# A fused FFT and expert kernel: late tiles by seven quarter products, result scatters in a queue of their own, gates zeroed first

## The chip, the cores and the metric

The kernel runs on one core of a Trainium2 chip. The metric is the device time of one execution in microseconds. A profiled execution comes with it: its span is the time from the first to the last recorded instruction, and the execution's own time is a little longer.

## The reference

Eight batches of 2496 tokens, 256 values each, are first filtered along the sequence with a Fourier transform, and the result goes through a mixture of eight experts, one expert a token, none dropped.

```python
X = np.fft.rfft(x, axis=1)
Y = X * (filt_r + 1j * filt_i)[None, :, :]
x = np.fft.irfft(Y, n=2496, axis=1).reshape(19968, 256)

logits = x @ w_gate                        # 256 x 8
expert_idx = np.argmax(logits, axis=1)
gate_w = softmax(logits)[arange(N), expert_idx]
for e in range(8):                         # rows of one expert
    h = np.maximum(x[rows of e] @ w1[e], 0.0)   # 256 -> 1024
    y[rows of e] = h @ w2[e]                    # 1024 -> 256
return gate_w[:, None] * y
```

All is float32. A float32 matmul appears in the profile as two MATMUL instructions, each with its LDWEIGHTS.

## The kernel before

The transform is a prime-factor one: 2496 = 39 x 64. For each batch, `stage_a` multiplies by the table tas (tile fin in, zo out, stored to zd in DRAM), `stage_b` by tbs and then by the filter ht (tiles ys and yw), `stage_c` by tcs (uo out, stored to ud) and `stage_d` by tds (yo out). The first batch stays in SBUF and is turned by TensorE instead (`first_a`, `turn_z`, `first_c`, `turn_u`; tiles zt, ut, zi, ui). The imaginary filter parts are multiplied by signs on GpSimd: `load_filters` lists the parts in `signs`, and `turn_z` works the list off. The gate weights lie in two padded tiles, wg (for the logits of batches 0 to 2) and wb (for the later ones); `load_rest`, one step at 0.8 of slot 0, zeroes them on VectorE and loads them, the row ids and the valid mask through the Sync queue. `make_constants` runs before all steps.

`route` finds each token's expert and its place among the expert's rows, and `scatter` writes the row with its id and gate to the DRAM tile rows by an indirect DMA of GpSimd. After each batch `tile_map` cuts the new rows into tiles of 512, 256 or 128 rows of one expert each: 65 tiles, of which 28 have 512 rows (tiles 1 and 7 to 33), then eight of 256 (34 to 41) and 23 of 128 (from `SHORT` = 42; `PLACE` = 34).

A tile's first product (x by w1, relu, into the two tiles hT) has two halves, one w1 transfer each. For 512 rows and for the last batch's 256 rows it is done `hidden_by_quarters`: seven products of quarters in the place of eight, with sums of x (`turn_x`, tile sums) and of w1 (`w1_sums`, tile wsum) made on GpSimd and the outputs added up on VectorE. The second product is `result(i, j)`: for each 128 rows, eight matmuls of 128 x 128 by 128 x 256, one scaling by the gate on VectorE or ScalarE into ys (four buffers), and at once an indirect DMA on GpSimd, which scatters the 128 rows into the output. It takes w2 from w2t (two buffers, one for each half) or, from tile `PLACE` on, from w2s, which holds all of w2. In the last batch `result` also issues the pad scatters of `pad_rows`, one a call.

The order of all instructions on each engine is written out by a planner when the program is built. The class `Order` keeps a clock for each engine and an estimate of when each tile is ready. The main loop picks the next step for TensorE among the open transform steps and the heads of two streams, `first_products` and `second_products`; `when(key)` says when a head could start. Two streams that are both ready alternate. After each step `flush` issues stores that are due, `more_loads` the transform's loads, `side` the routing work, and `prefetch` the expert tiles' rows and weights and the w1 sums. The odd half of tile i's first product waits until the second product of tile i - 1 is over (`ends`). When the transform and the routing are over, `late` is filled: the transform's SBUF is given back and w2s and eight more w1 buffers (w1b) are placed there; w2s loads start at once. Each engine and each queue works its instructions off in the order in which they were issued. All instructions pass through the helper `Issue`, so nearly every one carries line 243.

Of the kernel before, what the change touches and what calls it, by code (L numbers as in the profile page):

```python
# [124 lines left out]
class Order:  # L125
# [5 lines left out]
    def __init__(self, nc):  # L131
        self.nc = nc
        self.t = dict.fromkeys(("tensor", "vector", "scalar", "gpsimd", "sync", "transfers"), 0.0)
        self.slow = self.busy = self.last = 0.0
        self.lands = [0.0] * 8
        self.done, self.used, self.slots, self.ahead = {}, {}, {}, {}
        self.tensor, self.vector, self.scalar, self.gpsimd, self.sync = (
            Issue(self, name) for name in ("tensor", "vector", "scalar", "gpsimd", "sync"))
# [37 lines left out]
        return size / n * packet / 14e3 * (1.7 if n >= 1024 and (in_ if out.space == DRAM else out).ap[0][1] <= 64 else 1.0)  # L176

    def count(self, engine, op, args, named):
        aps = [a for a in list(args) + list(named.values()) if isinstance(a, bass.AP)]
        if not aps:  # L180
            return
        out, ins = aps[0], aps[1:]
        if "out" in named:
            out = named["out"]
            ins = [a for a in aps if a is not out]
        if op.endswith("value_load"):
            out, ins = None, aps
        at = named.get("out_offset")
        if at is not None:
            ins.append(at.ap)  # L190
        kept = [a for a in ins if a.space != DRAM or a.name[:2] in ("zd", "ud")]
        free = self.t[engine]
        start = max([free] + [self.ready(a) + (self.HOP if engine != "sync" else 0.0) for a in kept])
        if out is not None:
            start = max(start, self.ahead.pop(out.name, 0.0))
            n = int(np.prod([d[1] for d in out.ap][1:])) if out.space != DRAM else 0
        tail = 0.0
        if op.endswith("dma_start"):
            busy = 1.03 if engine == "gpsimd" else 0.4
            if engine == "sync":  # L200
                start = max(start, self.lands[-8])
            self.t[engine] = start + busy
            took = self.transfer(out, named["in_"])
            self.t["transfers"] = max(self.t["transfers"], start + busy) + took
            end, tail = self.t["transfers"], self.LOAD
            if engine == "sync":
                self.lands = self.lands[-7:] + [end + tail]
        else:
            if out is None:
                took = 0.8 if engine == "sync" else 0.02  # L210
            elif engine == "tensor":
                if start > self.busy + 1.2:
                    self.slow = start + 3.4
                rows = out.ap[0][1]
                took = max(0.1, 0.00085 * n) if op == "transpose" else max(0.216, 0.00169 * n) if rows > 32 else 0.00045 * n
                took *= 2.0 if start < self.slow else 1.0
                tail = 0.25
            elif engine == "vector":
                took = 0.15 + n / 960
            elif engine == "scalar":  # L220
                took = 0.16 + n / 1200
            else:
                took = 0.2 + n / 480
            end = self.t[engine] = start + took
            if engine == "tensor":
                self.busy = end
        for a in kept:
            self.used[a.name] = max(self.used.get(a.name, 0.0), end)
        for key in self.parts(out) if out is not None else ():
            self.done[key] = max(self.done.get(key, 0.0), end + tail)  # L230
        self.last = end + tail
# [59 lines left out]
def kernel(  # L291
# [86 lines left out]
    vld = cst.tile([P, 2 * NG + 2], F32, name="vld")  # L378


    first = ExitStack()
    pro = open_pool(first, name="pro", bufs=2, side="right")
    tau_i = pro.tile([1, 32], I32, name="tau_i", bufs=1)
    e_i = pro.tile([P, E], I32, name="e_i", bufs=1)
# [49 lines left out]

    def load_rest():
        nc.sync.dma_start(out=tds, in_=td)
        nc.vector.memset(wg, 0.0)
        nc.sync.dma_start(out=wg[:, :, :E], in_=moe_w_gate.rearrange("(i p) e -> p i e", p=P))
        nc.vector.memset(wb, 0.0)
        for i in range(4):  # L440
            nc.sync.dma_start(out=wb[i * CT:(i + 1) * CT, :, i * E:(i + 1) * E], in_=moe_w_gate.rearrange("(j p) e -> p j e", p=CT))
        nc.sync.dma_start(out=ids0, in_=ids)
        nc.sync.dma_start(out=vld, in_=valid)

    def make_constants():
        make_identity(nc.nc, ident)
        nc.gpsimd.memset(ones, 1.0)
        nc.gpsimd.affine_select(
# [30 lines left out]
    NIN, YB = 7, 6  # L479
    sb.live["in"] = lambda: {tile.name for tile in ins.values()}  # L480

    moves, stored = [], set()

    def move(o, i):
        moves.append((i, lambda: nc.sync.dma_start(out=o, in_=i)))
# [4 lines left out]
    def flush():  # L490
        while moves and (moves[0][0] is None or nc.ready(moves[0][0]) <= t["tensor"] + 0.2):
            moves.pop(0)[1]()

    def fin(key):
        ins[key] = sb.tile([P, 4, D], F32, tag="in", name="fin", bufs=NIN)
# [128 lines left out]
    def turn_z(f):  # L624
        if f % 4 == 0:
            nc.scalar.copy(out=ht[HP:, f:f + 4], in_=ht[:HP, f:f + 4])
            while signs and signs[0][0] <= f // 4:
                _, part, sign = signs.pop(0)
                nc.gpsimd.tensor_tensor(part, part, sign, op=ALU.mult)
        zi = outs["zi", f] = pro.tile([P, 2, D], F32, tag="zi", name="zi")  # L630
# [219 lines left out]
            yield  # L850

    def scatter(key, at, what):
        sc = nc.gpsimd.indirect_dma_start(
            out=rowsd,
            out_offset=bass.IndirectOffsetOnAxis(ap=at, axis=0),
# [10 lines left out]
    def tile_map(b, rows, n, last):  # L866
# [19 lines left out]
        yield 3  # L886
        most = max(m for group in GROUPS for _, m in group)
        tau = pools["moe"].tile([1, most], F32, tag="tau", name="tau", bufs=1)[:, :n]
        past = pools["moe"].tile([P, D], F32, tag="ys", name="past", bufs=4)[0:1, :n * (E - 1)].rearrange("p (n e) -> p n e", e=E - 1)
        she = (1, n, E - 1)  # L890
        nc.vector.tensor_tensor(
# [39 lines left out]
    SHORT = next(i for i in range(NT) if TILES[i][0] == 1)  # L931

    PLACE = next(i for i in range(NT) if TILES[i] == (2, B - 1))
    late = {}

    def quarters(i):
# [23 lines left out]
    def weights(h, second):  # L960
# [10 lines left out]
            return  # L971
        ev = nc.sync.value_load(work[i][1], min_val=0, max_val=E - 1)
        if second:
            w2t[h] = pools["moe"].tile([P, FH2, D], F32, tag="w2t", name="w2t", bufs=2)
            nc.sync.dma_start(out=w2t[h], in_=moe_w2[bass.ds(ev, 1), k].rearrange("o p i d -> p (o i) d"))
        else:
            pool, bufs = (late["w1"], 8) if i >= SHORT else (pools["moe"], 3)
            w1t[h] = pool.tile([P, DH, 2, 2 * P], F32, tag="w1t", name="w1t", bufs=bufs)
            nc.sync.dma_start(out=w1t[h], in_=moe_w1[bass.ds(ev, 1), k].rearrange("o p i h f -> p (o i) h f"))
# [89 lines left out]
    def result(i, j):  # L1069
# [5 lines left out]
        p = bank()  # L1075
        for k in range(FT):
            w2 = late["w2s"][:, bass.ds(ev, 1), k, :] if i >= PLACE else w2t[2 * i + k // FH2][:, k % FH2, :]
            mm(p[:, :D], lhsT=hs[i][k % 4 // 2][:, k // 4, k % 2, j * P:(j + 1) * P], rhs=w2, start=(k == 0), stop=(k == FT - 1))
        ys = pools["moe"].tile([P, D], F32, tag="ys", name="ys", bufs=4)
        gate = gis[i][:, j, 8:9]  # L1080
        either(p, D, lambda: nc.vector.tensor_scalar(ys, in0=p[:, :D], scalar1=gate, scalar2=None, op0=ALU.mult),
               lambda: nc.scalar.activation(ys, p[:, :D], AF.Copy, scale=gate))
        nc.gpsimd.indirect_dma_start(
            out=out,
            out_offset=bass.IndirectOffsetOnAxis(ap=gis[i].bitcast(U32)[:, j, :1], axis=0),
            in_=ys,
            in_offset=None,
            bounds_check=N - 1,
            oob_is_err=False,
        )  # L1090


    sides = []

# [116 lines left out]
    def prefetch():  # L1211
# [6 lines left out]
        for what in ("w1", "w2"):  # L1218
            h = got[what]
            if h < 2 * min(len(work), NT - RARE) and rows_at[work[h // 2][3]] <= t["tensor"] and (  # L1220
                    h - used[what] < ((3 if h < 2 * SHORT else 8) if what == "w1" else 2 if h < 2 * PLACE else 8)):
                weights(h, what == "w2")
                asked.add((what, h))
                got[what] += 1
        for h in range(used["w1"], got["w1"]):
            if quarters(h // 2) and h not in wsum and len(wsum) < 2 and nc.ready(w1t[h]) <= max(t["tensor"], t["gpsimd"]) + 0.3:
                w1_sums(h)

    def when(key):

# [2 lines left out]
        if what == "w2":  # L1233
            if halves[0] <= n or key not in asked:
                return None
            return max(ps.free("bank"), nc.ready(*hs[i], *((late["w2s"],) if i >= PLACE else (w2t[2 * i], w2t[2 * i + 1]))))
        if key not in asked or what != "x" and n % 2 and ends[0] < i:
            return None
        if what == "x":
# [44 lines left out]
    def second_products():  # L1284

        for i in range(NT - RARE):
            for j in range(TILES[i][0]):
                yield lambda: result(i, j), 3.42, ("w2", 2 * i + 1)
            hs.pop(i), gis.pop(i), w2t.pop(2 * i, None), w2t.pop(2 * i + 1, None)
            used["w2"] += 2  # L1290
            ends[0] += 1

    def rare_tiles():

        for i in range(NT - RARE, NT):
# [4 lines left out]
            for h in (2 * i, 2 * i + 1):  # L1300
                for a in range(4):
                    hidden(i, h % 2, a)
            result(i, 0)

    def share():

# [5 lines left out]
    with tc.manual_schedule(engines=None):  # L1312
# [35 lines left out]
        while fs or any(heads):  # L1348
# [27 lines left out]
            if not fs and not sides and not late:  # L1376
                fft.close()
                tail = late["tail"] = open_pool(ctx, name="tail", bufs=1)
                late["w1"] = open_pool(ctx, name="w1b", bufs=8)
                late["n"] = 0  # L1380
                late["pads"] = pad_rows()
                late["w2s"] = tail.tile([P, E, FT, D], F32, name="w2s")
            prefetch()
            if used["x"] > SHORT and "need" not in late:
                late["need"] = nc.values_load(need, min_val=0, max_val=GROUPS[-1][-1][1])
        with tc.If(late["need"] > GROUPS[-1][-1][1] - RARE):  # L1386
            rare_tiles()

# [29 lines left out]
```

## Time and profile before

| | us |
|---|---|
| median of 3 runs | 1496.89 (1492.83 to 1498.1) |
| the profiled execution's own time | 1495.25 |
| its span | 1493.5 |
| TensorE busy (matmul) | 1456.2 |
| VectorE busy | 767.1 |
| GpSimd busy | 732.0 |
| ScalarE busy | 471.5 |

A row of the profile names engine, operation, the tile written and the tiles read, the shapes and the number of instructions; then busy time, mean duration, and the idle time before such instructions with what ended it. Busy time of TensorE counts overlapping instructions once. PEld is its weight load, SPq the Sync engine's DMA queue, POOL is GpSimd, DVE VectorE, ACT ScalarE.

### The profile page before, as it was taken

What the parts mean: (1) busy time and instruction counts of PE and PEld (TensorE: products, weight loads), DVE (VectorE), ACT (ScalarE), POOL (GpSimd) and SP (SyncE); (2) the same over time, 40 slices, a digit from 0 to 9 for tenths busy, and PEclk for the clock granted to TensorE, in tenths of its full rate; (3) what the DMA queues carried; (4) which work ended last, traced back from release to release, by engine and by line L of the source; (5) the groups of instructions that cost most, each with busy time, mean ns of one, the idle gap of its engine ahead of it and who ended that gap; (6) DMA issues with size and microseconds to landing.
All of it is one profiled execution on the core that took longest, in us unless ns stands there. A gap on an engine that the chain in (4) does not pass through costs nothing. (4 is left out here: it accounts for less than half of the span.)

```text
span 1493.5 us, 24437 instructions
## 1 busy us (share of the span) xinstructions
PE 1456.2 (98%) x7396; PEld 1149.4 (77%) x7396; DVE 767.1 (51%) x1731; ACT 471.5 (32%) x984; POOL 732.0 (49%) x1053
## 2 busy tenths in 40 slices
PE   8898999999999999999999999999999999999998
PEld 6453556767677767777778788887888889999997
DVE  4567669255765665567756545437344344441110
ACT  4454542333332233322222322222222222223332
POOL 3434455355545554555466565664546455741111
PEclk9899999999999999999999999999999999999999
DMA  9649898787875576547355535545455543356661
GB/s 262 203 150 326 288 324 265 229 272 224 293 213 175 153 266 179 161 130 251 106 138 167 176 113 143 125 150 150 149 178 172 170 146 107 112 190 178 182 180 51
DMA packets 216376, 278.10 MB, mean 186 GB/s; under 512 B 124131, under 2 KB 163708, under 8 KB 216245
## 3 DMA queue, kind: packets, MB, share of 16 engines
q1 hardware_dynamic: 197125, 233.19, 52.4%
q0 software_dynamic: 19120, 43.33, 8.4%
q8 instruction: 62, 1.02, 0.3%
q14 instruction: 69, 0.57, 0.1%
HBM read 196.45 MB, written 80.64 MB: 186 GB/s over the span
## 5 line engine op out<-in xcount | busy, mean ns | idle before, releaser
L243 PE MATMUL bank<-w2t,hT 128*128 128x256 f32 x1984 | 446.4, 381 | 1.0 <-DVE hT L243 1.0
L243 DVE TENSOR_TENSOR hT<-bank,hT 128x512 f32<-128x512 f32 (+1 forms) x504 | 300.9, 626 | 277.9 <-PE bank L243 157.8
L243 PEld LDWEIGHTS bank<-w2t,hT 128*128 128x128 f32 x1984 | 376.2, 191 | 64.2 <-issue 10.6
L243 POOL DMA_INDIRECT out_dram<-ys,ng x161 | 160.7, 998 | 473.4 <-ACT ys L243 181.0
L243 PE MATMUL bank<-xT,w1t 128*128 128x256 f32 (+1 forms) x1728 | 316.6, 329 | 0.0
L243 PEld LDWEIGHTS bank<-xT,w1t 128*128 128x128 f32 x1728 | 267.2, 192 | 30.8 <-issue 6.5
L243 ACT ACTIVATE hT<-hT 128x1024 f32<-128x1024 f32 (+1 forms) x144 | 134.6, 960 | 375.1 <-DVE hT L243 364.1
L243 POOL DMA_INDIRECT rows<-yo,row x176 | 180.5, 1026 | 68.5 <-POOL yo L243 28.7
L243 ACT ACTIVATE ys<-bank,ng 128x256 f32<-128x256 f32 x121 | 57.4, 474 | 365.3 <-PE bank L243 311.0
L243 PE MATMUL bank<-sums,wsum 128*128 128x256 f32 (+1 forms) x576 | 135.7, 358 | 0.0
L243 PE MATMUL bank<-w2s,hT 128*128 x592 | 132.6, 379 | 0.0
L243 PEld LDWEIGHTS bank<-w2s,hT 128*128 128x128 f32 x592 | 110.3, 190 | 13.8
L243 PEld LDWEIGHTS bank<-sums,wsum 128*128 128x128 f32 x576 | 100.9, 190 | 20.0 <-issue 9.6
L243 DVE TENSOR_TENSOR ys<-bank,ht 128x512 f32<-128x512 f32 x80 | 54.9, 686 | 64.4 <-PE bank L243 59.8
L243 PE MATMUL bank<-fin,tas 117*120 117x512 f32 x154 | 77.7, 624 | 10.5 <-DMA fin<-in_x_dram 9.9
L243 DVE STREAM_TRANSPOSE xT<-xg 128x512 f32<-128x512 f32 (+2 forms) x126 | 57.5, 495 | 57.1 <-PE bank L243 56.1
L243 PE MATMUL bank<-fin,tds 120*128 120x512 f32 (+1 forms) x168 | 74.9, 565 | 4.3 <-DMA fin<-ud 4.1
L243 PE MATMUL bank<-ys,tcs 128*128 128x512 f32 x140 | 73.9, 613 | 4.1 <-DVE yw L243 3.4
L243 POOL TENSOR_TENSOR wsum<-w1t 128x256 f32<-128x256 f32 x72 | 53.6, 745 | 48.6 <-PE bank L243 45.7
L243 PE MATMUL bank<-fin,tbs 128*128 128x512 f32 x140 | 73.4, 611 | 2.0 <-DMA fin<-zd 2.0
L243 ACT ACTIVATE hT<-bank 128x128 f32<-128x128 f32 (+1 forms) x191 | 57.7, 304 | 53.0 <-PE bank L243 45.0
L243 PE MATMUL bank<-xT,wsum 128*128 128x256 f32 (+1 forms) x288 | 68.9, 362 | 1.9 <-DVE hT L243 1.9
(150 smaller groups left out, 1492.7 us busy)
## 6 DMA issues: line engine op xcount, KB each, us to landing
w1t<-in_moe_w_dram SPq DMA_DIRECT2D x126, 512.0 KB
w2t<-in_moe_w_dram SPq DMA_DIRECT2D x68, 512.0 KB
fin<-in_x_dram SPq DMA_DIRECT2D x39, 512.0 KB
fin<-zd SPq DMA_DIRECT2D x35, 512.0 KB
ud<-uo SPq DMA_DIRECT2D x35, 512.0 KB
fin<-ud SPq DMA_DIRECT2D x35, 512.0 KB
zd<-zo SPq DMA_DIRECT2D x35, 480.0 KB
xg<-rows SPq DMA_DIRECT2D x112, 128.0 KB
```

The source lines that it names most:

```text
L243: return real(*args, **named)
```

## The change

It has four parts.

First, the second product of a 512-row tile that begins when `late` is filled is made by `result_by_quarters`: the product 512 x 1024 by 1024 x 256 is cut into two halves of rows, of the inner dimension and of columns, and seven products of quarters (two times four matmuls of 128 columns each) take the place of eight. `h_sums` makes the sums of hT on VectorE (three adds of 128 x 1024; a fourth in the steps), `w2_sums` those of w2 on GpSimd (four of 128 x 512, one at a time between other work). Outputs are added up on VectorE and scaled on ScalarE. w2t gets two more buffers in a pool `quads`, which is closed after the last such tile (`LARGE` = 34) and whose place w1b then takes. The host lays w2 out so that the first half of the inner dimension is the first half of hT; `result` reads hT in that order for all tiles.

Second, `result` no longer issues its scatter: `deliver` puts it into a list, and `send` issues it when the planner takes the rows to be ready, or when more than three wait. Output scatters are declared free of order among themselves. Where a scatter would directly follow another on GpSimd, a memset of one element's width goes between them.

Third, the zeroing of wg and wb moves from `load_rest` to the start of `make_constants`.

Fourth, `turn_z` applies the signs of one more group of filter rows.

```diff
     def load_rest():
         nc.sync.dma_start(out=tds, in_=td)
-        nc.vector.memset(wg, 0.0)
         nc.sync.dma_start(out=wg[:, :, :E], ...)
-        nc.vector.memset(wb, 0.0)
...
     def make_constants():
+        nc.vector.memset(wg, 0.0)
+        nc.vector.memset(wb, 0.0)
         make_identity(nc.nc, ident)
...
     def flush():
...
+        while sends and (nc.ready(sends[0][0]) <= t["tensor"] + 0.2 or len(sends) > 3):
+            send()
...
-            while signs and signs[0][0] <= f // 4:
+            while signs and signs[0][0] <= f // 4 + 1:
...
     def scatter(key, at, what):
+        if nc.sent:
+            nc.gpsimd.memset(tau0[:, 31:], 0.0)
...
+            w2t[h] = (late["quads"] if late and late["flip"] else pools["moe"]).tile([P, FH2, D], F32, tag="w2t", name="w2t", bufs=2)
...
-        nc.gpsimd.indirect_dma_start(out=out, ...)
+        deliver(i, j, ys)
+
+    def send():
+        ys, ng, j = sends.pop(0)
+        if nc.sent:
+            nc.gpsimd.memset(tau0[:, 31:], 0.0)
+        sc = nc.gpsimd.indirect_dma_start(out=out, ...)
+        tc.declare_no_dep(sc.ins, group="results", reason="rows of their own")
+        tc.add_to_no_dep_group("results", sc.ins)
...
+    def h_sums(i):
+        a = [t.rearrange("p f v (r c) -> p r (f v) c", r=2) for t in hs[i]]
+        ss = hsum[i] = [late["quads"].tile([P, FH2, 2 * P], F32, tag="hsum", name="hsum", bufs=3) for _ in range(2)]
+        nc.vector.tensor_tensor(ss[0], a[0][:, 1], a[1][:, 1], op=ALU.add)
+        nc.vector.tensor_tensor(ss[1], ss[0], a[0][:, 0], op=ALU.subtract)
+        nc.vector.tensor_tensor(a[0][:, 1], a[0][:, 0], a[0][:, 1], op=ALU.subtract)
+
+    def w2_sums(i):
+        w = [w2t[2 * i + g].rearrange("p k (n d) -> p n k d", n=2) for g in range(2)]
+        ts = late["quads"].tile([P, 3, FH2, P], F32, tag="tsum", name="tsum", bufs=2)
+        nc.gpsimd.tensor_tensor(ts[:, 0], w[0][:, 1], w[0][:, 0], op=ALU.subtract)
+        yield
+        nc.gpsimd.tensor_tensor(ts[:, 1], w[1][:, 1], ts[:, 0], op=ALU.subtract)
+        yield
+        nc.gpsimd.tensor_tensor(ts[:, 2], w[1][:, 0], ts[:, 1], op=ALU.subtract)
+        yield
+        nc.gpsimd.tensor_tensor(w[0][:, 1], w[1][:, 1], w[0][:, 1], op=ALU.subtract)
+        tsum[i] = ts
+
+    def result_by_quarters(i):
...
+        def product(left, right):
+            q = bank()[:, :D].rearrange("p (j d) -> p j d", j=2)
+            for j in range(2):
+                for k in range(FH2):
+                    mm(q[:, j], lhsT=left[:, k, j * P:(j + 1) * P], rhs=right[:, k], start=k == 0, stop=k == FH2 - 1)
+            return q
...
+        q = product(a[0][:, 0], w[0][:, 0])
+        nc.scalar.copy(out=one, in_=q)
+        yield
+        q = product(a[1][:, 0], w[1][:, 0])
+        add(top[:, :, 0], q, one)
+        yield
+        ss, ts = hsum[i], tsum[i]
+        q = product(ss[1], ts[:, 1])
+        add(two, q, one)
+        nc.vector.tensor_tensor(a[1][:, 0], a[1][:, 0], ss[1], op=ALU.subtract)
+        yield
+        q = product(a[0][:, 1], w[0][:, 1])
+        add(three, q, two)
+        yield
+        q = product(ss[0], ts[:, 0])
+        add(low[:, :, 1], q, three)
+        add(four, q, two)
+        yield
+        q = product(a[1][:, 1], ts[:, 2])
+        add(low[:, :, 0], q, three)
+        for j in range(2):
+            send(2 + j, low[:, j])
+        yield
+        q = product(a[1][:, 0], w[1][:, 1])
+        add(top[:, :, 1], q, four)
+        for j in range(2):
+            send(j, top[:, j])
+        yield
...
     def second_products():
         for i in range(NT - RARE):
+            if late and i < LARGE:
+                wide.add(i)
...
+                for j in range(7):
+                    yield go, 1.79, ("wide", 2 * i + 1)
+            else:
...
             ends[0] += 1
+            if ends[0] == LARGE:
+                quads.close()
```

In `result_by_quarters` the inner `send(j, y)` takes a ys buffer, scales on ScalarE and calls `deliver`. `prefetch` issues `h_sums` once both hT tiles of the tile are ready, and one step of `w2_sums` at a time, for the tile at hand or the next, when GpSimd's clock is not more than 0.5 us ahead of TensorE's.

## The prediction

> **What bounds the kernel now.** I read the page first, then windows of the late stage, then TensorE's order of time at both ends of the run, then the waits of the places where TensorE stood still.
>
> ```profile
> PE 1456.2 (98%) x7396; PEld 1149.4 (77%) x7396; DVE 767.1 (51%) x1731; ACT 471.5 (32%) x984; POOL 732.0 (49%) x1053
> PEclk9899999999999999999999999999999999999999
> DMA  9649898787875576547355535545455543356661
> ```
>
> TensorE is busy for 98% of the span, so time falls only if TensorE gets less work or loses one of its few gaps. Those gaps (about 37 us) lie before 320 us, around 1014 to 1033 us and after the last matmul at 1487 us. The third digit of the DMA row (75 to 112 us) is slack, the next four are not.
>
> The late stage, in TensorE's order of time (start and duration in us, then the instruction and how many):
>
> ```profile
> 1220.61 1.05 PE L243 MATMUL bank<-xT,w1t 128*128 128x128 f32 x8
> ...
> 1223.29 0.61 PE L243 MATMUL bank<-xT,wsum 128*128 128x128 f32 x4
> 1223.74 13.98 PE L243 MATMUL bank<-w2t,hT 128*128 128x256 f32 x64
> 1237.55 1.05 PE L243 MATMUL bank<-xT,w1t 128*128 128x128 f32 x8
> ```
>
> One 512-row second product is 64 instructions (32 matmuls of 256 columns, two instructions each) from 1223.74 to 1237.55 us: 13.81 us, 215.8 ns each. The 28 instructions of 128 columns from 1220.61 to 1223.74 us take 111.8 ns each. Half the columns cost 51.8% of the time.
>
> ```profile
> core 0: us, PE busy (x) PEld busy (x) DVE busy (x) ACT busy (x) POOL busy (x), PEclk, DMA share, GB/s
> 1148.09:1173.99 25.90, 25.90 (x121) 22.80 (x120) 10.91 (x18) 6.60 (x9) 16.32 (x21) 1.00 0.54 176
> ```
>
> This row of the windows holds one tile (span, then busy time by engine). A tile repeats every 25.90 us without a gap; VectorE is busy 10.9 us of it and GpSimd 12.2 to 16.8 us, so both have room.
>
> The start, TensorE and then the Sync queue (each line: start, duration, instruction, and in brackets the idle time before it and what ended it):
>
> ```profile
> 48.77 1.06 PE L243 MATMUL bank<-tcs,ys 128*128 128x128 f32 x8
> 56.05 3.74 PE L243 MATMUL bank<-fin,tas 117*120 117x512 f32 x4 [6.23 <-DMA fin<-in_x_dram]
> 59.58 1.91 PE L243 MATMUL bank<-tcs,ys 128*128 128x128 f32 x8
> 62.12 2.05 PE L243 MATMUL bank<-fin,tbs 128*128 128x512 f32 x2 [0.63 <-DMA fin<-zd]
> ```
>
> ```profile
> 41.53 0.47 SPq L243 DMA_DIRECT2D tds<-in_td_dram  x1
> 48.44 0.40 SPq L243 DMA_DIRECT2D wg<-in_moe_w_gate_dram  x1
> ...
> 51.78 0.38 SPq L243 DMA_DIRECT2D fin<-in_x_dram  x1
> ```
>
> The Sync queue stands from 42.0 to 48.4 us: its waits give 6.6 us to VectorE's wb, the memset that `load_rest` issues behind VectorE's filter products. The x load behind it goes out at 51.78 us, lands for 56.05 us, and TensorE stands 6.23 us. Then the four 512-column instructions take 3.53 us where they took 1.72 us elsewhere (25.89 us): from 56.05 to 66.55 us, work of 5.2 us (6 x 0.43 + 24 x 0.11) took 10.5 us. That is the 8 in the clock row's second digit.
>
> Third, GpSimd and VectorE before 304 us:
>
> ```profile
> 299.49 0.98 POOL L243 DMA_INDIRECT out_dram<-ys,ng  x1 [5.94 <-ACT hT L243]
> ```
>
> ```profile
> 300.71 0.20 DVE L243 TENSOR_REDUCE rs<-ex 117x6 f32<-117x48 f32 x1 [17.24 <-POOL yo L243]
> ```
>
> A result scatter waits 5.94 us in GpSimd's queue for its rows; a routing copy behind it ends 300.7 us, VectorE has waited 17.24 us for it, and TensorE waits 2.29 us at 303.96 us for the transpose behind that. The next instructions run slowly until 309 us, about 2 us more.
>
> **What the Trainium skill says.** "TensorE: Matmul & The Clock Gate", Part 1 on the clock gate: after an idle window of some 3.4 us the clock halves until a busy window has passed. The trace agrees: half rate after the 6.23 us gap. The same page, "LDWEIGHTS (loading the stationary operand)": a load takes columns over 1.2, 107 ns for 128, whatever streams past. So 128-column matmuls sit just above the load rate; the measured 111.8 ns says that the load is still hidden, and no narrower split would be. "SBUF — State Buffer", "Who interferes with whom": a VectorE instruction with two SBUF inputs and a GpSimd instruction that reads SBUF exclude each other. The trace agrees: VectorE's ys<-ys,yw takes 691 ns at least and 1269 ns at most, 0.58 us more, most of a GpSimd add (0.73 us).
>
> **The change part by part.**
>
> *Seven products (less work).* 8 x 8 matmuls of half-width, seven times: 7 x 2 x 4 x 2 = 112 instructions of 128 columns, 112 x 111.8 ns = 12.52 us against 13.81: 1.29 us a tile. It holds for tiles with `late` set before their second product: w2s loads begin at 1024.1 us, tile 25 is then in its second product, and the last 512-row tile is 33. Eight whole products follow (1045.36, 1070.39, ... 1223.74 us). 8 x 1.29 = 10.3 us. If the plan turns late one tile sooner or later, 1.3 us more or less.
>
> *Its sums, beside TensorE.* VectorE: four adds of 1024 elements; by slope from 421 ns (256) and 685 ns (512), 1.22 us each, and seven of 256 from a bank at 0.42: 7.8 us, less one scaling of 0.48 that now goes to ScalarE; 10.9 + 7.3 = 18.2 of 24.6 us. GpSimd: four of 512 at 1.27 us (its ys row): 5.1, for 12.4 + 5.1 = 17.5, and less still, since the eight pad scatters (0.99 each) ride on `result` and move to the 256-row tiles. ScalarE: one copy of 0.36 and one more scaling of 0.47. None of this is on TensorE's path unless late. The wait to look at is the third product's, for `hsum`: after the second half of a tile its relu is out about 2.1 us later; two adds make 4.5 us; with a GpSimd add ahead of each (0.73) about 6. Before it TensorE has products 1 and 2 (3.6 us) and two steps of the next tile's first half (3.4), 7.0 us. Behind the sums on VectorE stand the adds that free banks; seven banks cover about 3 us of backlog. The weight sums are made a tile ahead, from four w2t buffers instead of two. I take 0.8 us of loss in all: 9.5 us (bounds: 11.6, and below nothing as in the rival).
>
> *Gates zeroed first.* Two memsets, 0.112 and 0.272 us, move to VectorE's idle first microseconds. The five gate loads, ids and valid then follow tds directly and take the 3.34 us of before, so the x load goes at about 45.3 us and lands (4.27 us as before) at 49.6, in time for 49.83. The DMA engines are free for it: 0.13 busy from 45 to 52 us. Late next is fin<-zd: its stores of the last chunk go out by 46.5 instead of 53, but the Sync queue also holds the store of the chunk after, evacuated at about 49.6; so z is asked for at 50.1 instead of 56.6, used 5.5 us later at 55.6, while TensorE comes at 52.4. It stands 3.2 us and again loses some clock. Gain at that point 62.12 - 55.6 = 6.5 us, half-clock about even. Bounds: 11.5 (6.23 + 5.3, all of it) and 0 (crowded DMA after 112 us takes it back). I take 6.
>
> *Signs ahead.* The same five GpSimd groups (1.9 to 2.15 us), 7 us sooner, ahead of the ys adds in its queue. VectorE's waits for them (9.1 us in four) go. TensorE is saturated from 23.3 to 49.8 us, so nothing alone; without it the last ys, ready at 56.6 us, would take back the gain above. The filter parts are issued on SP 8 us ahead or more. Taken as 0 beside that gain.
>
> *Scatters queued late and unordered.* The same count of 0.99 us scatters; 181 us of GpSimd's waits for ScalarE's ys and 56 us for earlier scatters shrink, a memset of about 0.1 us between neighbours is added. Almost all lies beside TensorE. At 304 us it is worth 2.29 + 2.0 = 4.3 us at most; I take 3 and 0 as bound. The last scatter still follows the last matmul: nothing there. Later w1b buffers are wanted only from tile 38 on, when the late pool has closed: 0.
>
> Sum: 9.5 + 6 + 3 = 18.5 us. Against the profiled execution (span 1493.5, 1495.25 with what lies around) 1476.7; the median of the runs is 1.64 above that one, so **1478.4 us**.
>
> **Rivals.**
> *Stalls only shift (20%).* The z load or full DMA from 112 to 240 us (0.84 to 1.01 busy in most windows) gives back the start, the 304 us gap reappears in a changed plan. For it: VectorE is 75 to 97% busy there. Only 9.5 to 10 us stay: 1487.
> *VectorE and GpSimd share the new sums badly (7%; slower).* Place: the third product of each of eight tiles. If all three VectorE sums each wait for a 1.27 us GpSimd sum, hsum is done 2.1 + 3 x 2.49 = 9.6 us after the relu's start against 7.0: 2.6 us of standing, perhaps 1.5 of half clock, less 1.29: +2.8 x 8 = 22.5, less 9 from the start: 1510. It decides from 2.4 us a tile. Against it: weight sums come a tile ahead, and other GpSimd sums are 0.73.
> *It doesn't reach the tiles or the plan shuffles new gaps in (8%).* The planner's clocks change everywhere; one 3 us gap with its clock costs 6 us. About 1492.
>
> **How the numbers follow.** The forecast has 65%, its own range 1468 to 1485. The range 1467 to 1491 takes in the first rival and the bounds. A measurement can tell about 0.5% (7.5 us): below 1489.4 is faster. Forecast and most of the first rival make 0.80; its rest and the last rival 0.12; slower 0.08.
>
> **What would show it.** Seven groups of 16 instructions at about 1.79 us each in the late stage and a tile period of 24.6 us, eight times; GpSimd near 17 and VectorE near 18 us of it. No Sync wait on wb, x used at 49.8 us, a gap of about 3 us at fin<-zd. No VectorE wait of 17 us before 300. Wrong if the period stays above 25.5 us, or if z is used after 60 us.

## The result, and the profile after

The changed kernel takes 1480.04 us (median of six executions, 1478.19 to 1485.58); the kernel before takes 1494.95 us beside it (six executions, 1492.83 to 1498.1). The ratio is 0.9902, 95% interval 0.9883 to 0.9922: by the ratio 14.7 us less (11.7 to 17.5). The forecast was 1478.4. The profiled execution went from a span of 1493.5 us to one of 1476.5, so the traces below explain 17.0 us.

The page after, busy time by engine, then the rows of the 40 slices:

```profile
PE 1440.1 (98%) x7828; PEld 1147.0 (78%) x7828; DVE 848.7 (57%) x1819; ACT 480.6 (33%) x1004; POOL 822.0 (56%) x1213
...
PEclk9999999999999999999999999999999999999999
DMA  9759889795985585556544735556655425456661
```

TensorE bounds the kernel as before. It is busy 16.1 us less with 432 more instructions (whole instructions replaced by halves), VectorE works 82 us more and GpSimd 90 us more. The 8 in the clock row is gone.

One tile of the late stage, TensorE in order of time:

```profile
1072.06 1.89 PE L246 MATMUL bank<-xT,w1t 128*128 128x256 f32 x8
...
1078.10 1.95 PE L246 MATMUL bank<-w2t,hT 128*128 128x128 f32 x16
...
1086.86 1.95 PE L246 MATMUL bank<-tsum,hsum 128*128 128x128 f32 x16
1088.64 1.03 PE L246 MATMUL bank<-xT,wsum 128*128 128x256 f32 x4
...
1094.86 1.95 PE L246 MATMUL bank<-w2t,hT 128*128 128x128 f32 x16
1096.65 1.68 PE L246 MATMUL bank<-xT,w1t 128*128 128x256 f32 x7
```

From the start of one step to the start of the next (1094.86 to 1096.65) are 1.79 us, which is 16 times 111.8 ns. No line has a bracket: nothing was waited for. The windows of two tiles (span, then busy time of PE, PEld, DVE, ACT and POOL):

```profile
1047.46:1072.06 24.60, 24.60 (x171) 23.16 (x170) 19.52 (x27) 7.25 (x11) 21.43 (x24) 1.00 0.61 174
1072.06:1096.65 24.59, 24.59 (x171) 23.14 (x169) 19.51 (x27) 7.25 (x11) 21.41 (x24) 1.00 0.56 173
```

The period is 24.59 us. GpSimd (fifth figure, 21.4) is nearer to it than the forecast's 17: 3.2 us are left.

The start, TensorE and then the Sync queue:

```profile
52.07 1.95 PE L246 MATMUL bank<-fin,tas 117*120 117x512 f32 x4
...
56.65 1.10 PE L246 MATMUL bank<-fin,tbs 128*128 128x512 f32 x2 [1.74 <-DMA fin<-zd]
```

```profile
41.79 0.47 SPq L246 DMA_DIRECT2D tds<-in_td_dram  x1
42.32 1.45 SPq L246 DMA_DIRECT2D wg<-in_moe_w_gate_dram  x1
...
47.92 0.38 SPq L246 DMA_DIRECT2D fin<-in_x_dram  x1
```

The gate loads follow tds at once, the x load goes out at 47.92 us instead of 51.78, x is used at 52.07 us without a wait (4 instructions in 1.95 us, where they took 3.74), and one wait of 1.74 us for z is left.

To see where the rest went, each stretch of the trace is split into TensorE's work (instructions times 0.43, 0.2158 or 0.1118 us for 512, 256 or 128 columns) and the loss, which is what remains of the stretch. The loss is not only standing still: it also holds slow instructions and those of other sizes (before the change TensorE stood for 1.8 of the 20.0 us between 400 and 1000 us), so the columns are to be compared with each other. Each is one execution, and six executions of the changed kernel lie 7 us apart: a difference of 1 or 2 us in one cell decides nothing. Estimated from six traces, in us:

| | before | gates and signs only | scatters only | after | after, scatters ordered | after, queue only when late |
|---|---|---|---|---|---|---|
| TensorE's work | 1407.0 | 1407.0 | 1407.0 | 1395.3 | 1394.1 | 1396.6 |
| loss 0 to 80 | 18.7 | 10.3 | 19.7 | 9.7 | 9.9 | 9.3 |
| 80 to 300 | 25.1 | 30.8 | 27.0 | 24.7 | 27.0 | 25.2 |
| 300 to 400 | 9.8 | 6.5 | 4.4 | 4.4 | 8.8 | 5.9 |
| 400 to 1000 | 20.0 | 19.7 | 31.1 | 30.9 | 35.1 | 20.3 |
| 1000 to 1200 | 5.4 | 3.7 | 0 | 0 | 21.8 | 1.5 |
| from 1200 | 0 | 0 | 0 | 3.4 | 28.3 | 0.1 |

Before to after: 11.7 us less work; the start gives 9.0, the 304 us gap 5.4 and the gaps near 1014 to 1033 us another 5.4; new small gaps take 10.9 between 400 and 1000 us and 3.4 near 1220 to 1280 us. With the other stretches that makes 17, the fall of the span. The fall in work is that of nine wide tiles (288 instructions bank<-tsum,hsum, 32 a tile), not eight: the late stage began one tile earlier.

The new gaps before 1000 us, in TensorE's order of time after the change:

```profile
685.62 1.10 PE L246 MATMUL bank<-ys,tcs 128*128 128x512 f32 x2 [1.11 <-DVE ys L246]
...
892.52 0.30 PE L246 MATMUL bank<-sel,ls 128*64 128x32 f32 x2 [1.40 <-issue]
...
979.92 1.10 PE L246 MATMUL bank<-sums,wsum 128*128 128x256 f32 x4 [1.48 <-DVE hT L246]
983.50 2.86 PE L246 MATMUL bank<-w2t,hT 128*128 128x256 f32 x12 [1.62 <-DVE hT L246]
```

These are the larger of them, waits of 1.1 to 1.6 us for VectorE or, at 892 us, for nothing that the profile shows. The runs below show which part of the change brings them.

### The profile page after: what moved, and what is told of

Read it like the earlier page. It is cut to its first block, busy times and chain, and to the rows that moved or that the text cites. A ratio compares the mean times of both kernels' runs of the same rounds, so it can differ in the third digit from the quotient of the medians.

```text
span 1476.5 us, 25693 instructions
## 1 busy us (share of the span) xinstructions
PE 1440.1 (98%) x7828; PEld 1147.0 (78%) x7828; DVE 848.7 (57%) x1819; ACT 480.6 (33%) x1004; POOL 822.0 (56%) x1213
## 4 chain that ended last, share of the span: by engine, by line
PE 85%; DVE 6%; DMA 4%; issue 3%; ACT 1%; POOL 0%; SPq 0%; DVEq 0%; POOLq 0%; ACTq 0%
PE bank L246 83%; DMA fin<-in_x_dram 2%; PE lt L246 2%; DVE hT L246 1%; DVE yw L246 1%; DVE ys L246 1%; DMA fin<-ud 1%; DMA fin<-zd 1%; DMA zd<-zo 1%; POOL out_dram L246 0%; DVE take L246 0%; ACT hT L246 0%; SPq L246 0%; DMA w1t<-in_moe_w_dram 0%; DMA xg<-rows 0%
## 5 line engine op out<-in xcount | busy, mean ns | idle before, releaser
L246 PE MATMUL bank<-w2t,hT 128*128 128x256 f32 (+1 forms) x1984 | 388.6, 350 | 1.6 <-DVE hT L246 1.6
L246 PEld LDWEIGHTS bank<-w2t,hT 128*128 128x128 f32 x1984 | 334.5, 190 | 49.9 <-issue 9.6
L246 POOL DMA_INDIRECT rows<-yo,row x176 | 181.9, 1033 | 70.8 <-POOL yo L246 31.3
L246 ACT ACTIVATE ys<-bank,ng 128x256 f32<-128x256 f32 x102 | 48.4, 475 | 287.4 <-PE bank L246 231.7
L246 POOL TENSOR_TENSOR wsum<-w1t 128x256 f32<-128x256 f32 x72 | 60.1, 835 | 114.5 <-PE bank L246 96.7
L246 ACT ACTIVATE hT<-bank 128x128 f32<-128x128 f32 (+1 forms) x191 | 57.2, 303 | 53.9 <-PE bank L246 45.3
```

What stands on the lines that cost most here:

```text
L246: return real(*args, **named)
```

## The experiments

The ratios are each against the kernel before on the same chip.

**First question: which part made the start faster?** My theory was that gates and signs only work together; the rival, that one of them does it alone.

```diff
 def load_rest():                            # gates alone, on the kernel before
-    nc.vector.memset(wg, 0.0)
...
-    nc.vector.memset(wb, 0.0)
...
 def make_constants():
+    nc.vector.memset(wg, 0.0)
+    nc.vector.memset(wb, 0.0)
```


> The kernel before with the two gate memsets at the start, and nothing else. Theory (both edits are needed at the start): the Sync queue no longer waits 6.6 us for wb and the 6.23 us gap at the x load goes, but VectorE still waits for the signs, so the last filter products, ready at 56.6 us before, come late and TensorE waits for them; it is at most 4 us ahead at 120 us, total gain 0 to 4 us. Rival (the gates alone do it): 8 to 10 us ahead at 120 us, total gain 7 to 10 us.

Measured: 1491.17 us, ratio 0.9959 (0.9943 to 0.9976), about 6 us less: between the two forecasts.

```diff
-            while signs and signs[0][0] <= f // 4:        # signs alone
+            while signs and signs[0][0] <= f // 4 + 1:
```


> The kernel before with the signs one group ahead, and nothing else. Theory: VectorE's 9 us of waits for the filter part shrink, the gates' memsets sit behind the filter products in VectorE's queue and are reached sooner, so the Sync queue waits 3 to 5 us in the place of 6.6; gain 2 to 4 us at 120 us. Rival (signs are hidden anyway): the gap at the x load stays 6.2 us, gain 0.

Measured: 1491.05 us, ratio 0.9961 (0.9946 to 0.9976), again about 6 us less. The rival's 0 is out, and it is more than the theory's 2 to 4, though the Sync queue's wait for wb fell from 6.6 to 4.8 us as the theory had it.

> The kernel before with both start edits. Theory: the start of the changed kernel, 9 to 10 us ahead at 120 us; the total gain is 8 to 10 us if the plan behind it stays as it was, and 0.5 to 0.65% in time. Rival (the DMA engines, 0.9 busy from 112 us on, give it back): under 5 us.

Both edits together: 1487.25 us, ratio 0.9936 (0.9917 to 0.9955), about 9.6 us less, as expected. The interval (6.7 to 12.4 us) would still allow 6 and 6 to make 12; TensorE's waits in the start tell why they overlap. Gates alone, then signs alone, then both:

```profile
53.08 1.95 PE L243 MATMUL bank<-fin,tas 117*120 117x512 f32 x4 [1.09 <-DMA fin<-in_x_dram]
59.23 1.10 PE L243 MATMUL bank<-fin,tbs 128*128 128x512 f32 x2 [3.30 <-DMA fin<-zd]
```

```profile
57.84 3.16 PE L243 MATMUL bank<-fin,tas 117*120 117x512 f32 x4 [2.23 <-DMA fin<-in_x_dram]
62.59 1.10 PE L243 MATMUL bank<-fin,tbs 128*128 128x512 f32 x2 [0.23 <-DMA fin<-zd]
```

```profile
57.30 1.10 PE L243 MATMUL bank<-fin,tbs 128*128 128x512 f32 x2 [1.74 <-DMA fin<-zd]
```

Either edit cuts the same 6.23 us wait for x, to 1.09 or 2.23 us, but in different ways. With the gates alone x is there sooner (used at 53.08 us instead of 56.05). With the signs alone it is used later (57.84), and the wait is short because TensorE comes to it only at 55.6 us: it has 72 instructions bank<-tcs,ys ahead of x instead of 56, some 1.8 us, and in this execution stood 2.6 us longer before them. What the signs add to the gates is the rest of that wait and part of the z wait (3.30 to 1.74): with the gates alone VectorE still waited 3.5 us for GpSimd's ht there, with both no more. So my theory fell: no edit needs the other, they share one gap.

**Second: what are the scatters worth by themselves?**

```diff
-        nc.gpsimd.indirect_dma_start(out=out, ...)      # on the kernel before
+        sends.append((ys, gis[i], j))    # send(), flush(): as in the change
...
```


> The kernel before with the result scatters queued late, unordered and with the memset between neighbours, and nothing else. Theory: GpSimd's waits for ys shrink by 60 us or more and the gap at 304 us goes (5 us with its half clock), but the changed plan opens small gaps between 400 and 1000 us worth about 6 us, so the total is within 3 us of the kernel before. Rival (no new gaps come from this part): 4 to 5 us faster.

Measured: 1499.7 us, ratio 1.0017 (1.0 to 1.0035). Nothing, as the theory had it. The windows show effects that cancel. Before, then scatters only (span, then PE busy):

```profile
300.00:400.00 100.00, 96.66 (x472) 67.26 (x471) 56.41 (x142) 33.00 (x81) 50.42 (x80) 0.98 0.79 251
400.00:1000.00 600.00, 598.19 (x2966) 470.78 (x2965) 362.36 (x762) 174.91 (x323) 344.53 (x498) 1.00 0.58 168
1000.00:1100.00 100.00, 97.07 (x441) 84.24 (x440) 54.69 (x128) 23.45 (x31) 50.55 (x66) 0.98 0.55 166
```

```profile
300.00:400.00 100.00, 100.00 (x488) 69.02 (x487) 52.32 (x115) 35.38 (x87) 43.71 (x74) 1.00 0.79 254
400.00:1000.00 600.00, 589.70 (x2921) 461.16 (x2920) 372.88 (x811) 173.71 (x321) 347.39 (x541) 1.00 0.57 168
1000.00:1100.00 100.00, 100.00 (x466) 88.01 (x465) 43.35 (x69) 26.32 (x36) 49.81 (x72) 1.00 0.57 170
```

The 304 us gap is gone (96.66 to 100.00), and so are the gaps near 1014 to 1033 us (97.07 to 100.00), which the prediction had listed but not priced; by the table each is worth 5.4 us with the slow instructions behind it. Between 400 and 1000 us TensorE stands 10.3 us instead of 1.8. The changed kernel has 589.63 in that stretch: these gaps came with the scatters.

**Third: are the seven products worth their 11.6 us, and do they need the rest?** The changed kernel with whole products (`if late and i < LARGE` becomes `if False`, and no sums):

> The changed kernel with eight whole second products in every tile (the seven-product path is switched off; gates, signs and scatters stay as changed). Theory: the products are worth 9 tiles x 1.29 = 11.6 us of TensorE's work and nothing else of the change depends on them, so this kernel takes 11.6 us more than the changed one: ratio to before 0.998 (0.996 to 0.9995), TensorE's work back at 1407 us; the small gaps at 1220 to 1280 us remain, since the scatters cause them. Rival: the seven products bring those late gaps with them (hT late behind the sums), and only 8 us are lost: ratio 0.9955 or less and no gap at 1220 to 1280 us.

Measured: 1484.36 us, ratio 0.9933 (0.991 to 0.9957), span 1484.0 against 1476.5. TensorE's work is back at 1407.0 us, so the products are worth 11.7 us of work. But the span rises by 7.5 only: the gaps from 1220 to 1280 us are absent, 3.4 us of the difference. The theory's ratio of 0.998 fell, and the number and the missing gaps are what the rival said; that the products bring those gaps by delaying hT is not shown, since four later runs have the products and not the gaps. So of the products' 11.7 us, 7.5 reached the end in the traces; the two ratios put it at 0.0031 of 1495, 4.6 us, with intervals wide enough for anything from 0 to 9.

**Fourth: order or queue?** Three runs take the scatter edit apart, with everything else of the change in place. The planner writes a new order for each, so the number of tiles with seven products also varies (eight with scatters at once, nine in the changed kernel, ten in the first run here), which is worth 1.3 us a tile.

```diff
-        if nc.sent:                       # queue kept, ordered again, no memset
-            nc.gpsimd.memset(tau0[:, 31:], 0.0)
...
-        tc.declare_no_dep(sc.ins, group="results", ...)
-        tc.add_to_no_dep_group("results", sc.ins)
```


> The changed kernel with its result scatters still queued late, but ordered one behind the other again and without the memset between two of them. Theory (close-set unordered scatters hold up VectorE's adds near 1220 to 1280 us): the 3.4 us lost there go, the gaps between 400 and 1100 us, which come of the late queue, stay: 2 to 4 us faster than the changed kernel, ratio to before 0.9865 to 0.989. Rival (the order costs GpSimd more than it saves): waits of out_dram<-ys on DMA come back, some 56 us of them, and routing copies stand behind them: 1 to 5 us slower than the changed kernel, ratio 0.991 to 0.994.

Measured: 1535.73 us, ratio 1.0283 (1.0259 to 1.0308): 55 us more than the changed kernel. Both expectations fell; the rival had the direction and a tenth of the size.

```diff
     def deliver(i, j, ys):                # no order, no queue: issued at once
         sends.append((ys, gis[i], j))
+        send()
```


> The changed kernel with each result scatter issued at once behind its scaling, as before the change, but without an order among them and with the memset. Theory: the late queue cured the gap at 304 us (5.4 us) and brought the new small gaps of 400 to 1100 us (5.4 us); both go back, and the time stays within 2 us of the changed kernel: ratio to before 0.989 to 0.9915. Rival (lack of order, not the queue, cured 304 us): the 304 us gap stays cured and the new gaps go: 4 to 6 us faster, ratio 0.986 to 0.9875.

Measured: 1479.7 us, ratio 0.9896 (0.9868 to 0.9924), like the changed kernel. From 400 to 1000 us TensorE is busy 599.23 of 600 us again. The number is the theory's, but by luck: the 304 us gap came back only in part (98.11 of 100 us busy), and what used up the gain was 7.5 us of standing from 1000 to 1100 us, which nobody had named. Over all traces, TensorE stands 7.9 to 12.7 us between 400 and 1000 us in the six whose scatters are queued from the start, and 0.8 to 2.4 us in the eight others: the queue brings those gaps.

> The changed kernel with the scatters wholly as before: at once, ordered, no memset. Only gates, signs and seven products are left of the change. Theory (the scatters bring nothing and cost 3.4 us at 1220 to 1280 us): the gap at 304 us returns, those of 400 to 1100 and of 1220 to 1280 us go, and the sum of the parts stands, 9.6 + 11.6 = 21 us off the time before: ratio 0.9855 to 0.988, faster than the changed kernel. Rival (the seven products need GpSimd free of waits for its weight sums, which the late queue provides): the third product waits for its sums in some tiles and the time is 3 us or more above the changed kernel, ratio 0.992 or more.

Scatters at once and ordered: 1527.94 us, ratio 1.0225 (1.0197 to 1.0254). My theory, that the sum of the parts would stand at 21 us less, was wrong by 55 us, and the rival was right on the direction: the seven products cannot do without the missing order. It was not right that the late queue provides it. In the total the queue is worth nothing here (1480.0 with, 1479.7 without it; with the order 1535.7 and 1527.9), the lack of order everything. (The memset left with the order in both runs; it takes 0.09 us.) GpSimd of the run with the ordered queue, one tile:

```profile
1191.59 0.99 POOL L246 DMA_INDIRECT out_dram<-ys,ng  x1
1194.85 0.97 POOL L246 DMA_INDIRECT out_dram<-ys,ng  x1 [2.26 <-DMA out_dram<-ys,ng]
1198.04 0.97 POOL L246 DMA_INDIRECT out_dram<-ys,ng  x1 [2.22 <-ACT hT L246]
1201.62 0.97 POOL L246 DMA_INDIRECT out_dram<-ys,ng  x1 [2.60 <-ACT ys L246]
...
1214.45 1.71 POOL L246 TENSOR_TENSOR wsum<-w1t,wsum 128x256 f32<-128x256 f32 x1
1216.12 2.25 POOL L246 TENSOR_TENSOR w2t<-w2t 128x512 f32<-128x512 f32 x1
1218.52 1.80 POOL L246 DMA_INDIRECT out_dram<-ys,ng  x1 [0.15 <-issue]
```

An ordered scatter stands until the one before has landed, so scatters follow 3.2 to 3.6 us apart. (The bracket names whichever release came last; from 1000 to 1300 us GpSimd waits 21 times, 61.8 us in all, for DMA out_dram<-ys,ng, and never in the changed kernel.) Four take 11.0 us of GpSimd (1191.59 to 1202.59), and the next tile's first scatter comes 26.9 us after this one's, with sums all the way between: GpSimd's own round is longer than TensorE's 24.6. Two of the sums in it, beside VectorE's new sums, take 1.71 and 2.25 us, where the same sums take 0.72 and 1.27 elsewhere; without these 2 us the round would be about 24.9 us (an estimate from this tile). TensorE's tiles, 24.6 us apart until 1076 us, then come 27 to 31 us apart. In the changed kernel the four scatters of a tile start 1.29 us apart:

```profile
1170.14 0.98 POOL L246 DMA_INDIRECT out_dram<-ys,ng  x1 [0.37 <-ACT ys L246]
1171.13 0.09 POOL L246 MEMSET tau<- 1x1 f32 x1
1171.42 0.99 POOL L246 DMA_INDIRECT out_dram<-ys,ng  x1 [0.21 <-issue]
```

What TensorE mostly waits for in the ordered run (29.1 of 36.7 us of waits from 1000 to 1320 us) is neither the new sums nor hsum, but the first product's weight sums, which stand behind the scatters in GpSimd's queue:

```profile
1213.86 1.13 PE L246 MATMUL bank<-sums,wsum 128*128 128x256 f32 x4 [1.56 <-POOL wsum L246]
...
1280.11 0.80 PE L246 MATMUL bank<-sums,wsum 128*128 128x128 f32 x4 [4.14 <-POOL wsum L246]
```

The Trainium skill, "DMA: Bandwidth & Descriptors", "Anatomy of one DMA — SWDGE (gpsimd) path", puts a fixed cost of about 2.0 us on such a DMA, most of it until the write is confirmed. The trace agrees roughly: in the run with the ordered queue a median of 2.8 us from issue to landing for the scatters between 1000 and 1300 us, 2.4 at least.

**Fifth: is GpSimd really the bound, and only late?** The run with the ordered queue, with GpSimd's four sums of w2 left out (plain weights in their place, so that the output is not the product, but TensorE's instructions are the same):

```diff
-        nc.gpsimd.tensor_tensor(ts[:, 0], w[0][:, 1], w[0][:, 0], op=ALU.subtract)   # and three more
...
-        q = product(ss[1], ts[:, 1])
+        q = product(ss[1], w[1][:, 0])    # the other two likewise
```


> The run with ordered scatters (1535.7 us), but with the four weight sums of each second product left out: the products that used them read plain weights in their place, so the same matmuls run on other numbers. Theory (in that run GpSimd is the bound of the late stage: four ordered scatters 3.2 to 3.7 us apart, 5.1 us of second-product sums, 5.8 us of first-product sums and 2 us of row sums, 27 us against a tile of 24.6): without the 5.1 us it fits again, 0 to 10 us above the changed kernel, ratio to before 0.990 to 0.998. Rival (the waits behind the ordered scatters are themselves what TensorE waits for, whatever else GpSimd does): the time stays above 1520 us, ratio 1.018 or more.

Measured: 1491.17 us, ratio 0.9964 (0.9951 to 0.9977): some 45 us less than the same kernel with the sums, though every scatter is still ordered, as the theory had it. The windows from 1000 to 1300 us:

```profile
1000.00:1100.00 100.00, 100.00 (x689) 94.22 (x688) 73.16 (x111) 30.06 (x45) 53.13 (x64) 1.00 0.57 170
1100.00:1200.00 100.00, 100.00 (x689) 94.22 (x689) 71.73 (x111) 28.91 (x44) 56.40 (x68) 1.00 0.47 136
1200.00:1300.00 100.00, 94.60 (x631) 87.53 (x630) 49.00 (x116) 25.02 (x51) 65.55 (x96) 0.98 0.38 107
```

Without 5.1 us of sums a tile TensorE does not stand once in 200 us, where the ordered run lost 21.8. Scatters and sums each fit; together they don't. How much of this is the sums' own 5.1 us and how much the slowing of sums seen above was not separated. After 1200 us 11.5 us stay lost, at the weight sums of the 256-row tiles; that was not followed further.

```diff
-        tc.declare_no_dep(sc.ins, ...)    # queue throughout, order only until late (memset likewise)
+        if late:
+            tc.declare_no_dep(sc.ins, ...)
```


> The changed kernel, scatters queued late throughout, but ordered (and without the memset) until the late stage begins near 1000 us; unordered with the memset after that. Theory (the order costs only where GpSimd also makes the weight sums of the second product, for there its time a tile passes 24.6 us): within 3 us of the changed kernel, ratio to before 0.988 to 0.992. Rival (the order costs everywhere, since each ordered scatter waits some 2.7 us for the one before): at least a third of the 55 us comes back, ratio 1.0 or more.

Measured: 1479.41 us, ratio 0.9894 (0.9872 to 0.9917), the changed kernel's time, as the theory had it. In the total the order costs only in the late stage, though the gap before 304 us is back in this trace (96.15 of the 100 us from 300 to 400 busy).

**Sixth: a better version.** At once costs no small gaps before 1000 us, and the queue starts the late stage without the 11 us that the run with scatters at once loses from 1000 to 1100 us. So: no order anywhere, and the queue late only.

```diff
     def deliver(i, j, ys):
         sends.append((ys, gis[i], j))
+        while sends and not (late and ends[0] < LARGE):     # other run: and not late
+            send()
```


> The changed kernel, scatters unordered, but queued late only while the tiles of seven products last; at all other times a scatter is issued at once. Theory (the late queue brings the small gaps of 400 to 1100 us by another plan, and those of 1220 to 1280 us by setting four scatters in a row): the first shrink by some 5 us and the second go (3.4 us), the gap before 304 us may return (up to 5.4 us): 2 to 8 us faster than the changed kernel, ratio to before 0.985 to 0.989. Rival (each plan has gaps of its own, whatever the queue does): within 2 us of the changed kernel, ratio 0.989 to 0.992.

Measured: 1472.98 us, ratio 0.984 (0.9817 to 0.9864), at the fast end of the theory or past it.

> The changed kernel, scatters unordered, issued at once until the late stage begins near 1000 us and queued from there to the end. Theory: as the run that queues for the seven products alone, but with the 3.4 us of small gaps at 1220 to 1280 us, so slower than that run by 2 to 4 us: ratio to before 0.987 to 0.991. Rival (the gaps at 1220 to 1280 us have nothing to do with the queue): the two runs agree within 1 us and both or neither show them.

Measured: 1472.37 us, ratio 0.9849 (0.9826 to 0.9872). Both beat the changed kernel, by 7 to 9 us (7.1 and 7.7 by the medians, 9.3 and 7.9 by the ratios), and agree with each other, so the theory of 2 to 4 us between them fell. The windows of the second, with the gaps of 400 to 1000 us nearly gone:

```profile
400.00:1000.00 600.00, 597.58 (x2965) 473.40 (x2964) 360.85 (x783) 170.82 (x316) 345.16 (x530) 1.00 0.56 165
```

This closes the sum of the first of these two runs: 0.016 of 1496.2 is 23.9 us, of which gates and signs are 9.6, eight tiles of seven products 10.3, and what is left, 4, lies within the fall of the loss at 300 to 400 and 1000 to 1200 us (15.2 to 9.4 us in its trace).

The rival of the last run was right on the gaps at 1220 to 1280 us: it queues to the end, sets scatters as closely, and is busy 99.96 of the 100 us from 1200 to 1300; the run with order only early is busy all 100. Of the traces in which TensorE doesn't wait there for weight sums, only the changed kernel's shows these gaps, such as

```profile
1224.23 7.14 PE L246 MATMUL bank<-w2s,hT 128*128 x32 [0.41 <-ACT hT L246]
```

Their cause stays open: they belong to neither the queue, the close scatters nor the seven products alone, and whether other executions have them was not seen.

## Why the prediction was right, step by step

**Products: right in kind, two terms off.** The 111.8 ns rate held for the halves (1.79 us a step) and so did the period (24.59 for 24.6). Nine tiles, not eight, made it 11.7 us instead of 10.3; the step had named that as its bound. The 0.8 us of loss became 0 in the wide tiles; 3.4 us came later, from a cause that stays open. One reading behind the rate isn't borne out: the prediction works with 107 ns for a weight load, and the traces record 190 to 192 ns for each of these, overlapping at one every 111.8 ns.

**Sums beside TensorE: right, with less room than counted.** The w2 sums took 1.27 us as priced. The two hsum adds took more than the 1.22 us worked out by slope:

```profile
L246 DVE TENSOR_TENSOR hsum<-hT 128x1024 f32<-128x1024 f32 x9 | 16.3, 1812 | 3.5 <-ACT hT L246 3.2 <-POOL w1t L246 0.3
...
L246 DVE TENSOR_TENSOR hsum<-hsum,hT 128x1024 f32<-128x1024 f32 x9 | 14.1, 1572 | 0.3
```

VectorE came to 19.5 us a tile (18.2 forecast), GpSimd to 21.4 (17.5). GpSimd's 3.9 us too much are four of its sixteen sums, which in each tile from 1047 to 1170 us take 1.59 to 1.72 us instead of 0.72 while VectorE makes its new sums (the last section shows such a pair). The prediction had named this exclusion, but priced it only in its slower rival.

**Start: right on the queue, 6 us was 9 to 9.6.** The queue's wait for wb went, but the loads behind it took 5.6 us (42.32 to 47.92), not "the 3.34 us of before", so the x load went out at 47.92 us and not at 45.3. TensorE did not wait for x all the same, because it had work until 52 us, with 16 more instructions ahead of x in the three traces with the signs. The next in line was z, as forecast, but TensorE reached it at 54.91 us, not 52.4, so the wait was 1.74 us and not 3.2. The term "half-clock about even" failed too: the four instructions on x went from 3.74 back to 1.95 us. Nor does the prediction's idle window of 3.4 us settle what a wait costs here: after 2.23 us (signs alone) four instructions took 3.16 us, after 3.30 us (gates alone) two took 1.10, the full rate. "Taken as 0" for the signs was wrong as a claim about the edit alone (6 us), and in the sum it hid that the signs help to cover the late x load.

**Scatters: the wrong step.** "I take 3" for the 304 us gap: the gap went, as forecast, and with it those near 1014 to 1033 us, which the prediction had put at nothing; but the late queue brought some 11 us of small gaps before 1000 us, so by itself the edit is worth nothing (ratio 1.0 to 1.0035). And "almost all lies beside TensorE" was true of the kernel before only. The step priced a scatter at 0.99 us of GpSimd and added 5.1 us of sums to the busy time of a tile; in the queue an ordered scatter takes 3.2 to 3.6 us. Counted that way, four scatters (11.0 us, the last not waiting), eight wsum instructions (5.8), the row sums (2 to 3) and the w2 sums (5.1) make 24 to 25 us against 24.6: no room at all, and the slowing beside VectorE's sums made it 26.9 in the ordered run. The missing order would have stood as the part that the products rest on. It is worth 55 us there.

**Rivals.** Stalls did shift, but neither at the start nor to the DMA engines: they came from the plan, between 400 and 1000 us, as the third rival had it. The slower rival named GpSimd and VectorE holding each other up at the third product: they do, but the third product doesn't wait for it. The real danger lay in GpSimd's queue, at the first product's weight sums, and the lack of order averted it. The forecast's 18.5 us and the measured 14.7 agree in part by luck: in the traces products and start came out larger by 5 us, the 304 us gap by 2.4, the gaps near 1014 to 1033 us gave 5.4 that nobody had counted, and the new gaps took 14.3 back.

## What to carry to other kernels

Count an engine's room in the time that its queue is taken, not in its busy time: a DMA issue that must wait for the one before costs the queue its landing time, and work added to that engine meets the sum of both. When a change has several parts, ask of each which other part would fail without it; a part that is worth nothing alone can carry the largest gain. And where a plan places everything, an edit far from the bound can pay for itself in one place and be charged in another, so look for the same gain with the edit confined to the stage that needs it.

## What the runs showed of the hardware

VectorE's two-input adds and GpSimd's sums held each other up in the late stage. GpSimd and then VectorE of the changed kernel:

```profile
1179.60 1.44 POOL L246 TENSOR_TENSOR sums<-xT 128x128 f32<-128x128 f32 x1
1181.12 1.32 POOL L246 TENSOR_TENSOR sums<-xT,sums 128x128 f32<-128x128 f32 x1
...
1183.79 0.45 POOL L246 TENSOR_TENSOR sums<-xT,sums 128x128 f32<-128x128 f32 x1
```

```profile
1178.91 1.81 DVE L246 TENSOR_TENSOR hsum<-hT 128x1024 f32<-128x1024 f32 x1 [0.80 <-ACT hT L246]
1180.76 1.36 DVE L246 TENSOR_TENSOR hsum<-hsum,hT 128x1024 f32<-128x1024 f32 x1
```

While the two hsum adds of 1.81 and 1.36 us ran (1178.91 to 1182.12 us), two of GpSimd's 128x128 sums took 1.44 and 1.32 us, where a later one took 0.45; the shortest VectorE add of this size took 1.22 us. The Trainium skill, "SBUF — State Buffer", "Who interferes with whom", says that the two share a port pair under an exclusive lock; the trace fits, with both sides paying. In the changed kernel none of it reached TensorE, which is busy throughout from 1100 to 1200 us; in the ordered run it added about 2 us to the round of a GpSimd that had no room left.
